# Unpacking w1 and w2 on three engines, ELU sums and every fourth gated product on ScalarE and GpSimd, and longer waits assumed in the scheduler's list

## The chip, the cores and the metric

The kernel is one program on 1 core of one Trainium2 chip. Its engines are called by the profile's names: PE is TensorE (matrix products), PEld its weight loads, DVE is VectorE, ACT is ScalarE, POOL is GpSimd, and SP issues the transfers. The metric is device time in microseconds (us); lower is better.

## What is computed

Top-k attention (32 largest of 576 scores a row) with 8 heads on 4 batches of 576 tokens, then an ELU layer, then a gated layer with two more products:

```python
def _attn_ref(q, k, v):                          # q, k, v: 4 x 8 x 576 x 64, float32
    scores = np.matmul(q, k.transpose(0, 1, 3, 2)) / np.sqrt(D)
    kth = np.partition(scores, -32, axis=-1)[..., -32:-31]
    scores = np.where(scores >= kth, scores, -1e9)
    attn = np.exp(scores - np.max(scores, axis=-1, keepdims=True))
    attn = attn / (np.sum(attn, axis=-1, keepdims=True) + 1e-09)
    return np.matmul(attn, v)

def _moe_ref(x, w_in, w_out):                    # x: 2304 x 512, d_ff 2048
    h = x @ w_in
    return np.where(h > 0, h, np.exp(np.minimum(h, 0)) - 1) @ w_out

def _moe2_ref(x, w1, w2, w3, w_out):             # 512 -> 1024, 1024 -> 1024, 1024 -> 512
    return (((x @ w1) * (x @ w2)) @ w3) @ w_out
```

The weights are float64 on the host and reach the kernel as pairs of 32-bit words.

## The kernel before, in words

**Tiles and chunks.** The 2304 tokens are 18 tiles of 128; `CHUNKS` makes 9 chunks of 2 tiles. Attention works on a tile and a pair of heads at a time, 72 such steps in all, called attention tiles below: 8 to a chunk. The layers behind attention (`mlp`) work on a chunk of 256 tokens.

**One attention tile.** PE computes the scores of one head into the single buffer `psS` (L376). ACT copies them to SBUF (L382). DVE finds the 32 largest by four MAX8 (L389) with three MATCH_REPLACE8 between them (L392), per head. ACT makes the masked exponentials (L409, L411) and their fp16 high half `pi` (L426), POOL the low half (L427), SP transposes them into `pt` (L429), PE multiplies with the values (L442, 28 matmuls, called AV below), DVE scales by the sum (L447), ACT and POOL split the result in halves (L449, L450), and SP transposes it into the chunk's input `x` (L451).

**One chunk of the layers.** Every product is made of three fp16 products (high by high, high by low, low by high). `unitA` (8 a chunk, L674 to L676) multiplies x with w_in and makes the ELU: Relu of the negated product, Exp (ACT, L686 and L687), a scale (POOL, L689), and the sum of both branches. For chunks 0 and 1 (`gm0`, `gm1` are 0) the sum is one DVE instruction (L691); for the others (`gm` is 1) ACT makes a Relu (L695) and POOL adds (L696). ACT and POOL split the result (L697, L698). `unitO` (8 a chunk, L711 to L713) multiplies with w_out into `psY`. `y_evac` copies the output of the ELU layer (ACT L723, DVE L724); the first copy of chunk 0 is called the first output copy below. `unitB` (8 a chunk, L753 to L755) multiplies with w1 and w2; the gated product is an ACT copy (L772) and a DVE product (L773), and ACT and POOL split it (L778, L779). `unitD` (2 a chunk, L788 to L790) multiplies with w34, the product of w3 and w_out made once at the start.

**Weights.** `load64` brings 128 x 512 pairs of words and turns them into float32. With `whole` it takes three DVE instructions (L474 to L476); otherwise ACT scales the low words (L478), DVE joins the two (L479), ACT takes the sign (L480) and POOL adds (L481). Before the change w1 and w2 (16 pieces, `w12`) go by the first way, all others (56 pieces) by the second. A norm over each weight sets its scale; `convert` then splits each piece into halves (ACT L503, and DVE L506 or PE L515 and L516 with ACT L518).

**What sets the order.** All work is first listed as operations with an engine, an assumed cost and a priority (`Program.op`). `emit` plays the list through: an engine that is free takes the operation with the lowest rank (priority less `cpw` times the length of the path behind it) of those whose inputs would be there by the assumed costs and by the waits in `LAT`, the time from one engine's end to another's start. The program is then written out in that order, and each engine runs its own instructions strictly in it. The numbers in `PAR` are the priorities: `a0`, `a1` shift the first attention chunks, `lag0`, `lag` the layers behind attention, `pi`, `po`, `p12`, `p34` the loads of the weights, `ci`, `co`, `c12`, `c34` their conversion.

## Time and profile before

| | before |
|---|---|
| time, median of 3 runs | 1086.86 us (1085.69 to 1093.07) |
| time of the profiled execution | 1089.24 us |
| its span, first to last instruction | 1087.5 us |
| mean granted TensorE clock | 0.968 of 2.4 GHz |
| PE busy | 984.1 us (90%), 9132 matmuls |
| DVE busy | 921.6 us (85%), 2002 instructions |
| ACT busy | 834.9 us (77%), 1729 instructions |
| POOL busy | 661.2 us (61%), 689 instructions |

A busy time is the time that an engine had an instruction in work, as a share of the span. Matmuls overlap, so their listed durations add up to more than their engine's busy time; so do those of DVE and ACT to a smaller part, since an instruction's listed time begins a little before the one ahead of it has ended. A wait is put down to the instruction that came last by the profile. PEclk is the granted clock of TensorE as a share of 2.4 GHz.

### The profile page before, as it was taken

Reading aid. Unit: us, or ns where it says so; the run is one execution under the profiler, and the core shown is the slowest. Engines: PE = TensorE matmul, PEld = TensorE weight load, DVE = VectorE, ACT = ScalarE, POOL = GpSimd, SP = SyncE. Lnnn points to the kernel's source line nnn. Section 1 sums busy time; section 2 is a strip of 40 time slices with the busy share of each in tenths; the row PEclk is TensorE's granted clock in tenths of the full one; section 3 lists DMA queues with packets and bytes.
Section 4 is the critical chain, followed back from the end, with each engine's and each line's share of the span. In section 5 each row is a group of like instructions: output and inputs, shape, how many; then the busy total and the mean of one; then the engine's idle time right before and its main releaser. Section 6 shows DMA issues by size and latency. Waiting matters only on the chain.

```text
span 1087.5 us, 24859 instructions
## 1 busy us (share of the span) xinstructions
PE 984.1 (90%) x9132; PEld 780.0 (72%) x9132; DVE 921.6 (85%) x2002; ACT 834.9 (77%) x1729; POOL 661.2 (61%) x689
## 2 busy tenths in 40 slices
PE   3489847889889999999999999999999999999998
PEld 2244524569678868877886887788879869878875
DVE  6999999899999999999996999998799999951011
ACT  6878797697878867897896798788878967953522
POOL 4898862256357735974794597458738845852711
PEclk9989968799899999999999999999999999999999
DMA  9999996554458895467859657665864563230000
GB/s 363 296 316 316 303 275 169 159 130 112 120 144 163 191 231 149 101 166 198 187 134 237 168 116 144 174 183 124 207 160 113 133 159 81 68 84 11 2 20 20
DMA packets 262298, 174.65 MB, mean 161 GB/s; under 512 B 197408, under 2 KB 224032, under 8 KB 262176
## 3 DMA queue, kind: packets, MB, share of 16 engines
q1 hardware_dynamic: 262176, 173.07, 60.3%
q8 instruction: 71, 1.16, 0.5%
q14 instruction: 51, 0.42, 0.1%
HBM read 104.33 MB, written 21.50 MB: 116 GB/s over the span
## 4 chain that ended last, share of the span: by engine, by line
DVE 22%; PE 14%; ACT 10%; POOL 8%; issue 5%; DMA 5%; SPq 1%; POOLq 0%; ACTq 0%; DVEq 0%
DVE m L389 10%; DVE wk L392 9%; DMA pt<-pi 3%; POOL pi L427 2%; PE psR L753 2%; PE psR L755 2%; PE psR L754 2%; ACT pi L426 2%; POOL g L698 1%; POOL t L696 1%; ACT y L411 1%; ACT s L382 1%; PE psR L788 1%; DMA qr<-qd 1%; PE psR L790 1%
## 5 line engine op out<-in xcount | busy, mean ns | idle before, releaser
L389 DVE MAX8 m<-wk 128x8 f32<-128x576 f32 x432 | 312.5, 747 | 1.3
L427 POOL TENSOR_TENSOR pi<-y,pi 128x576 f16<-128x576 f32 x144 | 188.0, 1314 | 126.6 <-ACT pi L426 96.8
L392 DVE MATCH_REPLACE8 wk<-m,wk 128x576 f32<-128x576 f32 x288 | 212.4, 741 | 0.0
L712 PE MATMUL psY<-g,wout 128*128 128x256 f16 x576 | 157.5, 273 | 1.9 <-POOL g L698 1.9
L753 PE MATMUL psR<-x,w 128*128 128x256 f16 x576 | 158.5, 275 | 0.8 <-DVE t L773 0.8
L754 PE MATMUL psR<-x,w 128*128 128x256 f16 x576 | 158.2, 275 | 1.1 <-DVE x L724 1.1
L674 PE MATMUL psR<-x,win 128*128 128x256 f16 x576 | 158.6, 275 | 0.1
L755 PE MATMUL psR<-x,w 128*128 128x256 f16 x576 | 158.3, 275 | 0.0
L711 PE MATMUL psY<-g,wout 128*128 128x256 f16 x576 | 157.7, 274 | 0.4 <-ACT g L697 0.4
L676 PE MATMUL psR<-x,win 128*128 128x256 f16 x576 | 158.0, 274 | 0.0
L675 PE MATMUL psR<-x,win 128*128 128x256 f16 x576 | 158.0, 274 | 0.0
L713 PE MATMUL psY<-g,wout 128*128 128x256 f16 x576 | 157.6, 274 | 0.0
L376 PE MATMUL psS<-kt,qh 128*128 128x288 f32 x320 | 110.2, 359 | 38.6 <-ACT s L382 19.1
L411 ACT ACTIVATE y<-y,ty 128x576 f32<-128x576 f32 x144 | 110.7, 771 | 3.3 <-POOL ty L401 3.3
L382 ACT ACTIVATE s<-psS 128x576 f32<-128x576 f32 (+1 forms) x160 | 102.3, 640 | 12.3 <-PE psS L376 11.4
L409 ACT ACTIVATE y<-s,ty 128x576 f32<-128x576 f32 x144 | 107.1, 769 | 5.4 <-POOL pi L427 2.1
L389 DVE MAX8 m<-s 128x8 f32<-128x576 f32 x144 | 105.1, 746 | 6.4 <-ACT s L382 6.0
L392 DVE MATCH_REPLACE8 wk<-m,s 128x576 f32<-128x576 f32 x144 | 106.3, 741 | 0.0
L376 PEld LDWEIGHTS psS<-kt,qh 128*128 128x128 f32 x320 | 63.4, 198 | 54.5 <-ACT s L382 24.7
L442 PE MATMUL psA<-vv,pt 128*128 128x64 f16 (+1 forms) x2240 | 84.1, 196 | 17.2 <-DMA pt<-pi 17.1
L442 PEld LDWEIGHTS <-pt 128*128 128x128 f16 (+1 forms) x2240 | 77.6, 103 | 29.8 <-DMA pt<-pi 20.4
L426 ACT ACTIVATE pi<-y 128x576 f16<-128x576 f32 x144 | 95.2, 677 | 3.8 <-DMA pt<-pi 3.4
(167 smaller groups left out, 2426.8 us busy)
## 6 DMA issues: line engine op xcount, KB each, us to landing
kt<-kd SPq DMA_DIRECT2D x64, 288.0 KB, 3.3
vv<-vd SPq DMA_DIRECT2D x32, 448.0 KB, 4.6
qr<-qd SPq DMA_DIRECT2D x72, 128.0 KB, 3.0
raw<-kd SPq DMA_DIRECT2D x32, 288.0 KB, 4.2
kd<-kt SPq DMA_DIRECT2D x32, 288.0 KB, 3.9
wout<-w_in SPq DMA_DIRECT2D x16, 512.0 KB, 8.3
w<-w3t SPq DMA_DIRECT2D x16, 512.0 KB, 7.0
w<-w_out SPq DMA_DIRECT2D x16, 512.0 KB, 6.2
```

The lines of the kernel that those rows point to most:

```text
L376: T.matmul(psS[:, half, 0:288], lhsT=L[qs][:, hh], rhs=KT[kk][:, half * 288:half * 288 + 288], start=li == 0, stop=li == 1)
L389: op("DVE", 685, lambda r=r, src=src, m8=m8, hh=hh: V.max(m8[:, hh, 8 * r:8 * r + 8], src), [skey], [mk], p1 + PAR["ot"] * STEP)
L392: op("DVE", 677, lambda r=r, nsrc=nsrc, w=w, m8=m8, hh=hh: V.match_replace(w, m8[:, hh, 8 * r:8 * r + 8], nsrc, -3.0e38), [skey, mk], [k], ...
L427: op("POOL", 1234, lambda Y=Y, PIs=PIs: G.tensor_tensor(PIs[:, S:2 * S], Y, PIs[:, 0:S], op=OP.subtract), [yk], [("pi", ps)], p4 + .034 * ...
L442: T.matmul(psA[c0:c1, hs], lhsT=PT[pts[hh]][:, j, c0:c1], rhs=W[vs][:, j, hs], start=i == 0, stop=i == 13)
L674: T.matmul(o, lhsT=hi(W)[:, cs], rhs=X[:, 0, kd_, 0:N], start=kd_ == 0, stop=False)
L675: T.matmul(o, lhsT=hi(W)[:, cs], rhs=X[:, 1, kd_, 0:N], start=False, stop=False)
L676: T.matmul(o, lhsT=lo(W)[:, cs], rhs=X[:, 0, kd_, 0:N], start=False, stop=kd_ == 3)
L711: T.matmul(o, lhsT=hi(W)[:, cs], rhs=rh, start=ft == 0 and m % 2 == 0, stop=False, skip_group_check=True)
L753: T.matmul(o, lhsT=hi(W)[:, cs], rhs=X[:, 0, kd_, 0:N], start=kd_ == 0, stop=False)
L754: T.matmul(o, lhsT=hi(W)[:, cs], rhs=X[:, 1, kd_, 0:N], start=False, stop=False)
L755: T.matmul(o, lhsT=lo(W)[:, cs], rhs=X[:, 0, kd_, 0:N], start=False, stop=kd_ == 3)
```

## The change

- `whole` no longer holds `w12`: the 16 pieces of w1 and w2 are unpacked by ACT, DVE, ACT and POOL (L478 to L481), and `WORD` halves their scale.
- `gm0` and `gm1` go from 0 to 1: the ELU sums of chunks 0 and 1 (16 units) go by L695 and L696.
- `bm` goes from 0 to 4: in units B 0 and 4 of each chunk (18 in all) ACT copies both products in one instruction (L766) and POOL multiplies them (L770).
- The waits in `LAT` between different engines are about 1.8 times as long, the assumed rate of a transfer falls from 360 to 325 bytes a ns, a few assumed costs change, and nearly all priorities have other values.

The core of the diff (the assumed costs of QK, AV, MAX8, MATCH_REPLACE8, the weight product, the conversion, the transposes, the norm's products and a matmul are left out; the norm's rises by 27%, each other changes by 16% or less):

```diff
-LAT = {("ACT", "PE"): 285.0, ("POOL", "PE"): 210.0, ("DVE", "PE"): 200.0, ("PE", "ACT"): 197.0, ("PE", "DVE"): 197.0, ("ACT", "ACT"): 153.0,
+LAT = {("ACT", "PE"): 513.0, ("POOL", "PE"): 378.0, ("DVE", "PE"): 360.0, ("PE", "ACT"): 355.0, ("PE", "DVE"): 355.0, ("ACT", "ACT"): 153.0,
...
-PAR = dict(whole=('w12',), cd={'wi': [0, 0], 'wo': [0, 0], 'w34': [8, 0], 'w12': [16, 0]}, pv=116.655, pi=265.308, p34=113.061, po=180.969, p12=190.557, pis=199.858,
+PAR = dict(whole=(), cd={'wi': [0, 0], 'wo': [0, 0], 'w34': [8, 0], 'w12': [16, 0]}, pv=230.352, pi=214.696, p34=-22.369, po=324.064, p12=151.752, pis=458.007,
...
-           nr34=2, gm0=0, gm1=0, gm=1, bm=0, cpw=13.0, step=6600.0, pvb=-52.296)
+           nr34=2, gm0=1, gm1=1, gm=1, bm=4, cpw=15.929, step=6600.0, pvb=-214.285)
...
-        op("SP", nbytes / 360.0, lambda: Q.dma_start(dst, src), r, w, pr, lat=475.0)
+        op("SP", nbytes / 325.0, lambda: Q.dma_start(dst, src), r, w, pr, lat=475.0)
```

How the order moves, at three places. First DVE, where pieces of w1 and w2 are unpacked, at the 9th attention tile before and the 10th now; `w` is the weight buffer, `pp` the buffer in which raw words and later the gated products stand, `m`, `wk` and `s` belong to attention. Before:

```order
L479 SCALAR_TENSOR_TENSOR w_115<-w_115 128x512
L474 TENSOR_SCALAR w_115<-w_115 128x512 x2
L475 SCALAR_TENSOR_TENSOR w_115<-w_115 128x512 x2
L476 SCALAR_TENSOR_TENSOR w_115<-w_115 128x512 x2
L474 TENSOR_SCALAR w_115<-pp 128x512
L447 TENSOR_TENSOR xf_156<-psA,ty_166 128x128
L475 SCALAR_TENSOR_TENSOR w_115<-pp,w_115 128x512
L474 TENSOR_SCALAR w_115<-pp 128x512
L476 SCALAR_TENSOR_TENSOR w_115<-pp,w_115 128x512
```

After:

```order
L389 MAX m_161<-s_134 128x8
L389 MAX m_160<-wk_137 128x8
L479 SCALAR_TENSOR_TENSOR pp<-pp 128x512
L392 MATCH_REPLACE wk_137<-m_160,wk_137 128x576
L288 TENSOR_REDUCE sc<-psY_170 128x1
L389 MAX m_160<-wk_137 128x8
L479 SCALAR_TENSOR_TENSOR pp<-pp 128x512
L447 TENSOR_TENSOR xf_156<-psA,ty_166 128x128
```

Three DVE instructions a piece have become one, with attention's instructions between one piece and the next.

Second ACT, at the 9th attention tile, where w_out is converted (`wout`, from the result `psY` of PE). Before:

```order
L400 ACTIVATE ty_164<-m_160 128x2
L409 ACTIVATE y_138<-s_132,ty_164 128x576
L409 ACTIVATE y_139<-s_133,ty_164 128x576
L503 ACTIVATE wout<-wout,sc 128x512 x2
L518 ACTIVATE wout<-psY_171 128x512
L382 ACTIVATE s_132<-psS 128x576
L518 ACTIVATE wout<-psY_170 128x512
L411 ACTIVATE y_138,ty_164<-y_138,ty_164 128x576
```

After:

```order
L411 ACTIVATE y_139,ty_164<-y_139,ty_164 128x576
L449 ACTIVATE xt_155<-xf_156 128x128
L426 ACTIVATE pi_141<-y_139 128x576
L478 ACTIVATE pp<-pp 128x512
L480 ACTIVATE w_115<-pp 128x512
L503 ACTIVATE wout<-wout,sc 128x512
L413 ACTIVATE ty_164<-ty_164 128x2
L503 ACTIVATE wout<-wout,sc 128x512 x2
L478 ACTIVATE pp<-pp 128x512
L480 ACTIVATE w_115<-pp 128x512
```

The unpacking of w1 and w2 (L478, L480) now stands on ACT between attention's copies and the conversion of w_out. Of ACT's instructions, 418 stood ahead of the first output copy (L723) before, and 477 stand there now: 32 of the 59 more are L478 and L480, 8 are L695, and 19 are others, since attention is one tile to two further at that place.

Third PE, right behind the last AV. Before:

```order
L442 LDWEIGHTS pt_143
L442 MATMUL psA<-vv_131,pt_143 128x64
L788 LDWEIGHTS pp
L788 MATMUL psR_174<-w_116,pp 128x512
L789 LDWEIGHTS pp
```

After:

```order
L442 LDWEIGHTS pt_143
L442 MATMUL psA<-vv_131,pt_143 128x64
L753 LDWEIGHTS w_115
L753 MATMUL psR_173<-x_145,w_115 128x256
L754 LDWEIGHTS w_115
L754 MATMUL psR_173<-x_145,w_115 128x256
```

Before, 18 matmuls of unit D and all 192 of chunk 7's units B followed the last AV; now 48 of these B matmuls do, and the other 144 and the 18 stand ahead of it. Up to the 56th attention tile the PE work ahead of each AV is almost what it was.

## Rows read from the trace of the kernel before

**Rows 1.** Busy time by stretch: stretch, its length, each engine's busy time (instructions), PEclk, DMA share, GB/s.
```profile
0.00:163.20 163.20, 107.61 (x529) 59.49 (x529) 146.23 (x265) 133.10 (x255) 125.17 (x104) 0.91 0.98 312
163.20:284.40 121.20, 104.25 (x881) 75.76 (x882) 115.61 (x272) 95.04 (x194) 53.79 (x57) 0.91 0.55 140
284.40:973.90 689.50, 662.42 (x6821) 557.28 (x6821) 647.11 (x1435) 569.85 (x1217) 447.82 (x496) 0.99 0.62 152
973.90:1087.50 113.60, 109.83 (x904) 87.45 (x900) 12.68 (x33) 36.91 (x65) 34.41 (x33) 1.00 0.04 16
```
**Rows 2.** ACT in order of time around the first output copy: start, duration, instruction.
```profile
282.93 0.67 ACT L723 ACTIVATE x<-psY,sc 128x512 f16<-128x512 f32 x1
283.50 1.46 ACT L503 ACTIVATE w<-w,sc 128x512 f16<-128x512 f32 x2
```
**Rows 3.** PE in order of time: the first unit B, and the end of the last AV.
```profile
287.21 0.27 PE L753 MATMUL psR<-x,w 128*128 128x256 f16 x1
...
973.36 0.58 PE L442 MATMUL psA<-vv,pt 128*128 128x64 f16 x14 [0.16 <-DMA pt<-pi]
```
**Rows 4.** ACT's waits up to 284.4 us: in total, times, longest.
```profile
ACT qh L356 <- DMA qr<-qd: 8.6, 2, 5.5
ACT ty L400 <- DVE m L389: 7.2, 5, 2.9
ACT w L618 <- PE psY L614: 5.9, 3, 2.9
ACT wout L503 <- DVE sc L263: 5.8, 1, 5.8
```
**Rows 5.** DVE groups by line: count, busy us, mean ns of one, idle before them.
```profile
L479 DVE SCALAR_TENSOR_TENSOR w<-w 128x512 int32<-128x512 int32 x40 | 37.3, 938 | 2.8 <-ACT w L478 2.6
L773 DVE SCALAR_TENSOR_TENSOR t<-psR,sc,t 128x256 f32<-128x256 f32 x72 | 34.0, 475 | 34.5 <-ACT t L772 34.3
L691 DVE SCALAR_TENSOR_TENSOR t<-psR,sc,t 128x512 f32<-128x512 f32 x16 | 11.7, 739 | 2.2 <-POOL t L689 2.2
L475 DVE SCALAR_TENSOR_TENSOR w<-pp,w 128x512 int32<-128x512 int32 x10 | 7.1, 707 | 0.0
L476 DVE SCALAR_TENSOR_TENSOR w<-pp,w 128x512 int32<-128x512 int32 x10 | 6.8, 682 | 0.0
L474 DVE TENSOR_SCALAR w<-pp 128x512 int32<-128x512 int32 x10 | 4.4, 441 | 4.3 <-DMA pp<-w 3.0 <-POOL g L481 1.2
```
**Rows 6.** Line L479 by itself: duration min/median/max in ns, first and last start.
```profile
L479 DVE SCALAR_TENSOR_TENSOR w<-w x40: 667/694/1792, 11.0 to 166.9; 128x512 int32<-128x512 int32 x40
L479 DVE SCALAR_TENSOR_TENSOR wout<-wout x16: 671/1101/1798, 13.2 to 122.2; 128x512 int32<-128x512 int32 x16
```
**Rows 7.** ACT groups by line.
```profile
L695 ACT ACTIVATE t<-psR,sc 128x512 f32<-128x512 f32 x56 | 38.2, 682 | 0.4 <-POOL g L698 0.4
L772 ACT ACTIVATE t<-psR,sc 128x256 f32<-128x256 f32 x72 | 33.6, 466 | 39.2 <-PE psR L755 35.0 <-DVE sc L263 4.0
L478 ACT ACTIVATE w<-w 128x512 int32<-128x512 uint32 x40 | 27.0, 674 | 5.1 <-DMA w<-w_out 2.9 <-POOL pi L427 1.3 <-DMA w<-w 0.7
```
**Rows 8.** POOL groups by line.
```profile
L696 POOL TENSOR_TENSOR t<-t,t 128x512 f32<-128x512 f32 x56 | 71.4, 1276 | 2.3
L357 POOL TENSOR_TENSOR ql<-qr,qh 128x256 fp32r<-128x256 f32 x72 | 53.9, 748 | 24.7 <-ACT qh L356 24.6
L481 POOL TENSOR_TENSOR pp<-pp,w 128x512 int32<-128x512 int32 x16 | 24.8, 1561 | 2.8 <-DVE w L479 2.7
```
**Rows 9.** PE's waits from 284.4 to 973.9 us.
```profile
PE psA L442 <- DMA pt<-pi: 10.9, 16, 2.1
PE psS L376 <- ACT s L382: 8.5, 10, 1.9
```
**Rows 10.** Pieces of the chain that ended last: start, length, what.
```profile
870.85 0.80 PE psS L376 x4
...
875.56 0.82 PE psA L442 x28
```

More of the change, by code (lines that the diff above doesn't have):

```diff
@@ L23 @@
 DM, DFF, DH = 512, 2048, 1024
-CHUNKS = [2]*9
-LAT = {("ACT", "PE"): 285.0, ("POOL", "PE"): 210.0, ("DVE", "PE"): 200.0, ("PE", "ACT"): 197.0, ("PE", "DVE"): 197.0, ("ACT", "ACT"): 153.0,
-       ("ACT", "DVE"): 147.0, ("ACT", "POOL"): 175.0, ("DVE", "ACT"): 128.0, ("DVE", "DVE"): 127.0, ("DVE", "POOL"): 203.0, ("POOL", "ACT"): 75.0,
-       ("POOL", "DVE"): 60.0, ("POOL", "POOL"): 88.0, ("PE", "PE"): 0.0, **{(e, "SP"): 67.0 for e in ("PE", "ACT", "DVE", "POOL")}}
+CHUNKS = [2] * 9
+LAT = {("ACT", "PE"): 513.0, ("POOL", "PE"): 378.0, ("DVE", "PE"): 360.0, ("PE", "ACT"): 355.0, ("PE", "DVE"): 355.0, ("ACT", "ACT"): 153.0,
+       ("ACT", "DVE"): 265.0, ("ACT", "POOL"): 315.0, ("DVE", "ACT"): 230.0, ("DVE", "DVE"): 127.0, ("DVE", "POOL"): 365.0, ("POOL", "ACT"): 135.0,
+       ("POOL", "DVE"): 108.0, ("POOL", "POOL"): 88.0, ("PE", "PE"): 0.0, **{(e, "SP"): 67.0 for e in ("PE", "ACT", "DVE", "POOL")}}
 NXS = 2
 STEEP = 2.0 ** 100
-PAR = dict(whole=('w12',), cd={'wi': [0, 0], 'wo': [0, 0], 'w34': [8, 0], 'w12': [16, 0]}, pv=116.655, pi=265.308, p34=113.061, po=180.969, p12=190.557, pis=199.858,
-           pos=-94.236, p12s=-194.985, p34s=16.277, ci=202.374, co=66.783, cos=-57.999, c12=275.249, m34=-471.595, c34=-63.018, m34s=28.657, h34=2, oq=53.713, os=7.994,
-           ok=113.472, ot=242.797, orr=151.048, opp=-250.875, oa=-82.219, ost=0.618, a0=125.007, a1=-15.227, lag0=114.106, lag=21.439, ho=2, h12=0, h12c=7,
-           nr34=2, gm0=0, gm1=0, gm=1, bm=0, cpw=13.0, step=6600.0, pvb=-52.296)
+PAR = dict(whole=(), cd={'wi': [0, 0], 'wo': [0, 0], 'w34': [8, 0], 'w12': [16, 0]}, pv=230.352, pi=214.696, p34=-22.369, po=324.064, p12=151.752, pis=458.007,
+           pos=-341.301, p12s=-225.683, p34s=41.293, ci=319.03, co=146.49, cos=-451.25, c12=177.354, m34=-791.931, c34=-287.596, m34s=53.079, h34=2, oq=63.603, os=43.99,
+           ok=226.416, ot=389.564, orr=844.424, opp=-269.728, oa=-91.857, ost=-258.2, a0=93.413, a1=30.072, lag0=93.126, lag=31.769, ho=2, h12=0, h12c=7,
+           nr34=2, gm0=1, gm1=1, gm=1, bm=4, cpw=15.929, step=6600.0, pvb=-214.285)
 def conv_modes(n, d, g):
@@ L286, in gram @@
                     T.matmul(ps[0:w, o:o + w], lhsT=c, rhs=c, start=pi == 0 and j == 0, stop=pi == len(pieces) - 1, skip_group_check=True)
-            op("PE", 55 * (n + 127) // 128, gram, keys, [pk], pr)
+            op("PE", 70 * (n + 127) // 128, gram, keys, [pk], pr)
         op("DVE", 600, lambda: V.tensor_reduce(m, ps, axis=AX.X, op=OP.max), [pk], ["nm0"], pr)
@@ L388, in attention @@
                         src, skey = (sS, ("s", ss)) if r == 0 else (w, k)
-                        op("DVE", 685, lambda r=r, src=src, m8=m8, hh=hh: V.max(m8[:, hh, 8 * r:8 * r + 8], src), [skey], [mk], p1 + PAR["ot"] * STEP)
+                        op("DVE", 665, lambda r=r, src=src, m8=m8, hh=hh: V.max(m8[:, hh, 8 * r:8 * r + 8], src), [skey], [mk], p1 + PAR["ot"] * STEP)
                         if r < 3:
                             nsrc = sS if r == 0 else w
-                            op("DVE", 677, lambda r=r, nsrc=nsrc, w=w, m8=m8, hh=hh: V.match_replace(w, m8[:, hh, 8 * r:8 * r + 8], nsrc, -3.0e38),
+                            op("DVE", 727, lambda r=r, nsrc=nsrc, w=w, m8=m8, hh=hh: V.match_replace(w, m8[:, hh, 8 * r:8 * r + 8], nsrc, -3.0e38),
                                [skey, mk], [k], p1 + PAR["ot"] * STEP)
@@ L428, in attention @@
                        [yk], [("pi", ps)], p4 + .034 * STEP)
-                    op("SP", 1008, lambda PIs=PIs, pt=pt: Q.dma_start_transpose(out=PT[pt], in_=PIs), [("pi", ps)], [("pt", pt)], p4 - 1e6, lat=1406.0)
+                    op("SP", 1050, lambda PIs=PIs, pt=pt: Q.dma_start_transpose(out=PT[pt], in_=PIs), [("pi", ps)], [("pt", pt)], p4 - 1e6, lat=1406.0)
                 if t == 0:
@@ L516, in rest @@
             T.matmul(ps, lhsT=nident, rhs=hi(W[i]), start=False, stop=True)
-        op("PE", 1080, rest, [*skeys, (nm, i), ("si", sid), "ident"], [pk], pr)
+        op("PE", 1250, rest, [*skeys, (nm, i), ("si", sid), "ident"], [pk], pr)
         op("ACT", 480, lambda: A.activation(lo(W[i]), ps, AF.Copy), [pk], [(nm, i, "l")], pr)
@@ L613, in part @@
                     k = a * 4 + kk
-                    op("PE", 860, lambda w=w3[a][0], kk=kk, k=k: T.matmul(acc, lhsT=w[:, kk * 128:kk * 128 + 128], rhs=W4[k][0], start=k == 0, stop=k == 7),
+                    op("PE", 930, lambda w=w3[a][0], kk=kk, k=k: T.matmul(acc, lhsT=w[:, kk * 128:kk * 128 + 128], rhs=W4[k][0], start=k == 0, stop=k == 7),
                        w3[a][1] + W4[k][1], [ak], p1)
@@ L659, in mlp @@
         N = n * 128
-        nm = N / 2.4 + 3.0
+        nm = N / 2.4 + 3.2
         pr_of = lambda u: pr0 + u * span / 28.0
@@ L791, in unitD @@
                 ks = [("pp", 2 * q), ("pp", 2 * q + 1), ("w34", 2 * q), ("w34", 2 * q + 1)]
-                op("PE", 1305, mm, ks + [k + ("l",) for k in ks], [("rot", rs)], pr)
+                op("PE", 1325, mm, ks + [k + ("l",) for k in ks], [("rot", rs)], pr)
             ts = nxt("t2", NT2)
```

4 lines of the change are left out of this document (2 added, 2 removed).

## The prediction

> **What bounds the kernel now.** I read the busy times by stretch first, then what each engine waited for, then the prices of the instructions that the change adds and removes.
>
> DVE sets the pace until attention is over. Up to 284.4 us it is busy 146.23 and 115.61 us, all but 22.6, and from there to the last AV 647.11 of 689.50, or 94% [rows 1]. PE is nearly as full in that second part: 662.42 of 689.50, 27.1 idle, at a granted share of 0.99 [rows 1]. What is left after the last AV at 974 is PE alone, 109.83 us busy of 113.60 [rows 1, 3]. So the span is made of two things: the time at which PE gets its first work behind the ELU layer (the first output copy at 282.9, the first unit B at 287.2 [rows 2, 3]), and from then on PE's own work plus the little that it loses. DVE's load matters only through those losses.
>
> ACT has room at the start: 133.10 and 95.04 us busy up to 284.4, so 56.3 idle. In the middle it is at 569.85 of 689.50, 83%. POOL has 105.4 us idle up to 284.4 [rows 1].
>
> **What each edit costs, engine by engine.**
>
> *DVE.* A piece of w1 or w2 took 441 + 707 + 682 ns by L474 to L476, 1.83 us; 16 pieces are 29.3 us that go. Each now takes one L479, at 938 ns on the mean: 15.0 come [rows 5]. The 16 ELU sums of 739 ns (11.8) and 18 gated products of 475 (8.6) go [rows 5]. Net: 34.7 us less. Of this little shows ahead of the first output copy, since by the order attention is further along there: -29.3 + 15.0 - 5.9 (8 ELU sums), but 11 MAX8, 6 MATCH_REPLACE8 and 3 conversions more, which at 0.74 to 0.8 us each (the 740 ns of the instructions of that size [rows 5]) are about 15. That is -5. The other 30 us leave the time between the first output copy and the end (1 of them after the last AV).
>
> The price of L479 is uncertain, because it swings: 667 ns at the least, 1792 at the most, and a median of 694 on one buffer, 1101 on another [rows 6]. By the median of 694 the 16 cost 11.1 us, by that of 1101 17.6. I keep 15.0; both ends move DVE's sum by 4 us at most.
> The Trainium skill (SBUF — State Buffer, Who interferes with whom) gives a reason: a VectorE instruction with two SBUF inputs and a GpSimd one that reads SBUF exclude each other, so that the later waits out the earlier. The spread of 667 to 1792 ns agrees; by this rule the new ones, beside a fuller GpSimd, would lie at 1101, and the net saving would be 32 us instead of 34.7.
>
> *ACT.* 16 pieces at two passes of 674 ns (L480 has the same shape) are 21.6 us, 16 Relus of 682 are 10.9, and 18 double copies at 682 instead of 466 are 3.9 [rows 7]. Listed durations overlap: the output copy of 0.67 us is followed after 0.57 [rows 2], so 0.10 goes from each of 48 new instructions. Sum: 36.4 - 4.8 = 32 us more.
> Ahead of the first output copy stand 59 more instructions: 32 unpacking passes at 0.57 (18.4), 8 Relus at 0.58 (4.7), and 19 of attention and conversion at the mean of all of ACT, 834.9 us over 1729 (9.2). That is 32 us, against 56.3 idle.
>
> *POOL.* 16 adds of 1561 ns (25.0), 16 ELU adds of 1276 (20.4), and 18 products of 128 x 256 at the 748 ns of the subtraction of that size (13.5) [rows 8]. That is 59 us more, 35 of it ahead of the first output copy, beside 105.4 idle [rows 1]. I cost it at nothing there; if the cover fails, rival 3 has the price.
>
> *SP and DMA.* The bytes are the same. The raw buffers of w1 and w2 are freed by POOL instead of DVE and the last loads stand later in the order; the early stretch moves 312 GB/s at a busy share of 0.98, and only the next, at 0.55 [rows 1], takes these loads. No term.
>
> *The list.* Longer assumed waits put dependent instructions further apart. That cannot shorten an instruction; it can only take idle time from engines whose queue heads wait. Nothing else hides in it.
>
> **The sum.** First, the first output copy. Its place on ACT needs ACT's work ahead of it, 227 us (133.10 + 95.04 less the 1.5 behind its start [rows 1, 2]), plus 32, plus the idle time that remains. Of the 56.3 us, waits for the loads of q (8.6), for the weight product (5.9) and for a scale (5.8) stay [rows 4]: 20 us as the lower bound. The upper bound is all 56. Waits for MAX8 (7.2 [rows 4]) and much of the small rest fall away, since ACT is now the later one there; I take 33, nearer the lower end. 227 + 32 + 33 = 292, **9 us later** (bounds -4 and +32).
>
> Second, 16 score matmuls and two AV groups more stand ahead of the first unit B. They cost 4 x 0.80 + 2 x 0.82 [rows 10], **4.8 us** that do not come later.
>
> Third, PE's losses from there to the last AV: 27.1 idle, and 0.01 of 689.5 at the lower clock, 6.9: 34 us [rows 1]. DVE, which drops from 647 to about 618 of 689.5 (90%), no longer paces PE in most places. But 10.9 of the idle time waits for the transposes of `pt` and 8.5 for ACT's score copies [rows 9], and those are not DVE's work. Bounds: 0 and 34 back; I take about half, **18**.
>
> 1087.5 + 9 - 4.8 - 18 = 1073.7 us of span. The profiled execution took 1.7 us more than its span and lies 2.4 above the median of the runs: **1073 us**, 1.3% faster. Note what this says of attention's end: behind the last AV stand 162 matmuls fewer (144 of B, 18 of D), which at 109.83 us for 904 [rows 1] is 19.7 us. So the last AV would end at about 981 instead of 974, although the whole is shorter.
>
> **Rivals.**
>
> 1. *ACT takes DVE's place.* ACT gets its 32 us exactly where the layers of chunk 0 hang on it (conversions of w_out, of w1 and w2, the ELU), and its queue is in order: idle time is not filled if the head waits. For it: ACT's order now has the unpacking between attention and conversion, and ACT is ahead of DVE only by that idle time. Against: of the 56.3 us only 20 are waits that I can name as fixed, and 83% later leaves room. Price: 42 us stay idle, so the copy is 18 later, DVE waits for score copies in the following ten tiles, and PE gets 11 back: 1087.5 + 18 - 4.8 - 11, **1089 us**, no change.
> 2. *DVE's relief goes through whole.* The copy comes 4 us earlier, where DVE's order lets it, and PE gets all 27.1 of idle time back, at the same clock: 1087.5 - 4 - 4.8 - 27.1, **1051 us**. For it: DVE at 94%. Against: the waits for `pt` [rows 9].
> 3. *GpSimd gets in the way, and the kernel is slower.* The 35 us put on POOL ahead of the first output copy stand in front of attention's low halves (L427), for which the transposes and so AV wait. For it: POOL was at 125.17 of 163.20 at the start [rows 1]. Against: only 53.79 of the next 121.20. If none of it is hidden: 1087.5 + 35 - 4.8 - 11, **1106 us**. It decides from a copy 27 us later, at 310: then the kernel is over 1% slower with 11 back. The Trainium skill (GPSIMD Engine Reference, Engine selection) sends elementwise additions and products to VectorE, since GpSimd takes about twice as long with two inputs. The trace agrees in the price: 682 + 1276 ns in place of 739 [rows 5, 7, 8]; whether it counts hangs on which engine is late.
>
> **How the numbers follow.** My sum 0.45, rival 1 0.30, rival 2 0.12, rival 3 0.13. The sum's own range is 1060 to 1084 (copy 4 earlier to 20 later, PE 10 to 27 back, not all at once). The range of 1053 to 1101 leaves out about half of rival 2 and most of rival 3. A measurement of this kernel can tell about 1% from no change, so 1076 and 1098 are the limits: faster 0.47 (three quarters of the sum, rival 2), same 0.34 (the rest of the sum, most of rival 1), slower 0.19 (rival 3, the far end of rival 1).
>
> **What would show it.** Right: DVE about 887 us busy, ACT 867, POOL 720; the first output copy between 285 and 301; PE's idle time from there to the last AV near 15 instead of 27; the last AV near 981 with about 94 us behind it. DVE's waits for the score copies (L382) may rise to 20 us in all. Wrong in the first step if the copy is later than 305 or earlier than 280; wrong in the third if PE's losses stay at 34, which with the copy 9 us later gives no change. A DVE sum above 900 would mean that L479 pays for GpSimd's load.

## The result, and the profile after

The changed kernel takes 1072.6 us in the median of 4 runs (1069.03 to 1074.64), the kernel before 1087.01 beside it. The ratio is 0.9837, with a 95% interval of 0.9808 to 0.9866. The profiled execution has a span of 1072.9 us instead of 1087.5, and a mean granted clock of 0.978 instead of 0.968.

Busy times of the changed kernel, from the page:

```profile
PE 974.6 (91%) x9132; PEld 776.8 (72%) x9132; DVE 907.8 (85%) x1936; ACT 863.4 (80%) x1777; POOL 714.9 (67%) x739
```

Busy times by stretch, cut at the first output copy and at the last AV as [rows 1] is, in the same columns:

```profile
0.00:163.20 163.20, 105.84 (x528) 59.22 (x529) 147.82 (x254) 133.51 (x253) 127.77 (x100) 0.94 0.94 300
163.20:296.00 132.80, 109.50 (x913) 77.89 (x912) 121.85 (x271) 125.27 (x256) 87.93 (x90) 0.91 0.60 161
296.00:979.60 683.60, 669.74 (x6971) 568.83 (x6968) 630.79 (x1395) 572.28 (x1216) 465.62 (x517) 1.00 0.63 151
979.60:1072.90 93.30, 89.52 (x731) 70.89 (x728) 7.30 (x19) 32.34 (x55) 33.54 (x33) 1.00 0.04 13
```

The first output copy on ACT, which answers to [rows 2]:

```profile
295.99 0.69 ACT L723 ACTIVATE x<-psY,sc 128x512 f16<-128x512 f32 x1
```

PE in order of time: the first unit B and the last AV, as in [rows 3]:

```profile
298.27 0.27 PE L753 MATMUL psR<-x,w 128*128 128x256 f16 x1
...
978.62 0.98 PE L442 MATMUL psA<-vv,pt 128*128 128x64 f16 x28
```

For the account, the kernel before has to be cut at its own copy, 1.5 us earlier than in [rows 1]:

```profile
0.00:282.90 282.90, 211.27 (x1396) 134.68 (x1396) 260.34 (x531) 226.67 (x445) 178.96 (x160) 0.91 0.80 239
282.90:973.90 691.00, 663.00 (x6835) 557.84 (x6836) 648.61 (x1439) 571.32 (x1220) 447.82 (x496) 0.99 0.62 152
```

From these rows the 14.6 us of span come out whole. The copy is 13.1 later (296.0 against 282.9). PE has 4.1 more of its work behind it by then (215.34 against 211.27). From the copy to the last AV it stands idle 683.60 - 669.74 = 13.9 us instead of 691.00 - 663.00 = 28.0, so 14.1 come back. Behind the copy PE's busy time falls from 663.00 + 109.83 to 669.74 + 89.52, by 13.6; 4.1 of that is the work done earlier, and 9.5 is the same 9132 matmuls taking less time over the whole span. The mean granted clock, which rose, would give just that (984.1 x 0.968 / 0.978 = 974.0, and 974.6 was measured), but the same sum fails for a kernel in the same order: for unpack_held below it gives 974.6 x 0.978 / 0.973 = 979.6, and 973.3 was measured. So how much of the 9.5 is the clock is not shown; the last section has a reason why that mean is not to be leaned on. Sum: 13.1 - 4.1 - 14.1 - 9.5 = -14.6. The 20 us by which the stretch behind the last AV is shorter are not a gain by themselves: those matmuls now stand ahead of it.

What PE waits for between the copy and the last AV (in total, times, longest), against [rows 9]:

```profile
PE psA L442 <- DMA pt<-pi: 8.4, 13, 2.0
PE psS L376 <- DMA kt<-kd: 3.9, 2, 2.8
```

The waits for the score copies, 8.5 us before, are gone, and those for `pt` fell from 10.9 to 8.4.

### The profile page after: what moved, and what is told of

Its sections match the earlier page's. It is cut to its first block, busy times and chain, and to the rows that moved or that the text cites. A ratio compares the mean times of both kernels' runs of the same rounds, so it can differ in the third digit from the quotient of the medians.

```text
span 1072.9 us, 24950 instructions
## 1 busy us (share of the span) xinstructions
PE 974.6 (91%) x9132; PEld 776.8 (72%) x9132; DVE 907.8 (85%) x1936; ACT 863.4 (80%) x1777; POOL 714.9 (67%) x739
## 4 chain that ended last, share of the span: by engine, by line
PE 45%; ACT 16%; DVE 14%; DMA 10%; issue 9%; POOL 6%; SPq 1%; POOLq 0%; ACTq 0%; DVEq 0%
DMA pt<-pi 5%; DVE m L389 4%; PE psS L376 4%; DVE wk L392 4%; PE psR L753 4%; PE psR L754 4%; PE psR L755 4%; PE psR L674 4%; PE psR L676 4%; PE psR L675 4%; PE psA L442 3%; PE psY L711 3%; PE psY L712 3%; PE psY L713 3%; DVE w L479 2%
## 5 line engine op out<-in xcount | busy, mean ns | idle before, releaser
L389 DVE MAX8 m<-wk 128x8 f32<-128x576 f32 x432 | 314.1, 748 | 2.4
L376 PE MATMUL psS<-kt,qh 128*128 128x288 f32 x320 | 109.8, 358 | 37.0 <-POOL kt L308 25.1
L389 DVE MAX8 m<-s 128x8 f32<-128x576 f32 x144 | 105.9, 747 | 23.4 <-ACT s L382 22.8
L382 ACT ACTIVATE s<-psS 128x576 f32<-128x576 f32 (+1 forms) x160 | 102.7, 642 | 19.3 <-PE psS L376 18.1
L376 PEld LDWEIGHTS psS<-kt,qh 128*128 128x128 f32 x320 | 63.3, 198 | 49.6 <-POOL kt L308 27.6
```

What stands on the lines that cost most here:

```text
L376: T.matmul(psS[:, half, 0:288], lhsT=L[qs][:, hh], rhs=KT[kk][:, half * 288:half * 288 + 288], start=li == 0, stop=li == 1)
L389: op("DVE", 665, lambda r=r, src=src, m8=m8, hh=hh: V.max(m8[:, hh, 8 * r:8 * r + 8], src), [skey], [mk], p1 + PAR["ot"] * STEP)
```

## The experiments

All numbers of a profile are from one execution each; the ratios are from repeated runs beside the kernel before. "Copy" is the start of the first output copy, "idle" PE's idle time from there to the last AV, "DVE" its busy time in the same stretch with its share.

| kernel | ratio to before, 95% | span | copy | last AV | idle | DVE |
|---|---|---|---|---|---|---|
| before | 1 | 1087.5 | 282.9 | 973.9 | 28.0 | 648.6 (94%) |
| after | 0.9837 (0.9808 to 0.9866) | 1072.9 | 296.0 | 979.6 | 13.9 | 630.8 (92%) |
| work_only | 1.1048 (1.1 to 1.1095) | 1198.3 | 420.1 | 1086.1 | 26.7 | 560.4 (84%) |
| list_only | 1.0628 (1.0587 to 1.0669) | 1150.7 | 395.6 | 1058.5 | 7.7 | 588.4 (89%) |
| waits_only | 1.0192 (1.0122 to 1.0261) | 1105.7 | 302.1 | 994.8 | 28.8 | 641.3 (93%) |
| short_waits | 1.0782 (1.0718 to 1.0847) | 1168.6 | 407.0 | 1075.2 | 12.1 | 587.1 (88%) |
| nudge | 1.0056 (1.0033 to 1.0079) | 1092.1 | 305.8 | 998.8 | 19.0 | 643.2 (93%) |
| dve_less | 0.9972 (0.994 to 1.0004) | 1083.3 | 284.8 | 969.8 | 26.1 | 628.9 (92%) |
| dve_less_after | 0.9826 (0.9772 to 0.988) | 1065.5 | 297.2 | 972.3 | 7.0 | 609.7 (90%) |
| early_less | 0.9951 (0.9923 to 0.9978) | 1079.8 | 279.3 | 966.2 | 25.8 | 648.0 (94%) |
| unpack_held | 0.9999 (0.9975 to 1.0024) | 1085.9 | 312.3 | 992.7 | 11.9 | 632.5 (93%) |
| no_add | 0.9844 (0.9801 to 0.9888) | 1065.9 | 292.0 | 972.6 | 11.7 | 630.9 (93%) |
| no_add_scale | 0.981 (0.9765 to 0.9856) | 1064.0 | 290.7 | 970.7 | 11.2 | 631.8 (93%) |
| elu_less | 0.9825 (0.9785 to 0.9864) | 1064.3 | 294.1 | 971.1 | 9.2 | 631.0 (93%) |

In the first four runs, work_only to short_waits, the scheduler plays out a new order. In nudge it does too, from a number changed by half a per cent. In the last seven the order of either kernel is held, instruction by instruction, and some are left out or replaced.

How far two executions differ by themselves can be read from the same runs. The spans of the kernel before go from 1078.1 to 1090.8 in 19 executions, those of the changed kernel from 1067.2 to 1072.9 in four. In dve_less nothing ahead of the copy differs from the kernel before, yet the copy is 1.9 us later and DVE 4.0 us longer busy by then. Differences of that size between two profiles show nothing.

### Work alone, list alone

The kernel before with the changed work and its own numbers (work_only):

```diff
-PAR = dict(whole=('w12',), cd={'wi': [0, 0], 'wo': [0, 0], 'w34': [8, 0], 'w12': [16, 0]}, pv=116.655, pi=265.308, p34=113.061, po=180.969, p12=190.557, pis=199.858,
+PAR = dict(whole=(), cd={'wi': [0, 0], 'wo': [0, 0], 'w34': [8, 0], 'w12': [16, 0]}, pv=116.655, pi=265.308, p34=113.061, po=180.969, p12=190.557, pis=199.858,
...
-           nr34=2, gm0=0, gm1=0, gm=1, bm=0, cpw=13.0, step=6600.0, pvb=-52.296)
+           nr34=2, gm0=1, gm1=1, gm=1, bm=4, cpw=13.0, step=6600.0, pvb=-52.296)
```

> The three moves of work alone: w1 and w2 unpacked on three engines, ELU sums of chunks 0 and 1 and every fourth gated product on ScalarE and GpSimd, with all waits, costs and priorities of before. My theory is that the time comes from VectorE's relief behind the first output copy, less what ScalarE loses ahead of it. Then this alone gives most of the gain: 1074 to 1080 us, with PE idle for less than 20 us from the first output copy to the last AV (27.1 before), and that copy 8 to 20 us later than 282.9. The rival is that the new list of waits and priorities makes the gain, and that the moved work only costs: then 1087 to 1095 us and PE's idle time there stays at 25 us or more.

The changed kernel's numbers with the work of before (list_only) is the same edit to the changed kernel in the other direction: `whole=('w12',)`, `gm0=0`, `gm1=0`, `bm=0`.

> The other half: all waits, costs and priorities of after, and the work where it was before (w1 and w2 unpacked by VectorE in three instructions, ELU sums of chunks 0 and 1 and all gated products on VectorE). My theory: VectorE is as full as before, so PE loses 25 us or more behind the first output copy, and the time is 1081 to 1090 us. The rival that the list makes the gain: 1068 to 1076 us. If both halves give half each, the time is near 1080 us in both runs.

Measured: 10.5% and 6.3% slower, both far above every range that was expected. Each half by itself loses over 60 us, although together they gain 14. Both lose it ahead of the first output copy, which comes at 420.1 and 395.6. Line L389 ahead of the copy, in the kernel before, in work_only and in list_only (min/median/max in ns, first and last start; six such instructions make an attention tile):

```profile
L389 DVE MAX8 m<-wk x88: 730/746/761, 18.4 to 280.1; 128x8 f32<-128x576 f32 x88
```

```profile
L389 DVE MAX8 m<-wk x140: 732/747/764, 18.4 to 415.5; 128x8 f32<-128x576 f32 x140
```

```profile
L389 DVE MAX8 m<-wk x123: 734/746/762, 17.2 to 372.3; 128x8 f32<-128x576 f32 x123
```

Before, 14.7 attention tiles are through DVE at that point; in the half-changed kernels it is 23.3 and 20.5, so the chunk-0 layers have slipped behind six to nine more attention tiles, where a chunk has eight. No instruction has become dearer (746, 747 and 746 ns): the list plays the same kind of work in another order. In the middle the two part. Busy times from the copy to the last AV, work_only and then list_only:

```profile
420.10:1086.10 666.00, 639.32 (x6503) 538.82 (x6504) 560.39 (x1220) 514.30 (x1084) 428.08 (x474) 0.99 0.54 131
```

```profile
395.60:1058.50 662.90, 655.18 (x6718) 555.47 (x6717) 588.40 (x1307) 525.46 (x1121) 420.70 (x466) 1.00 0.57 139
```

With the lighter DVE (84%) and the list of before PE idles 26.7 us, about as much as before. With the heavier one (89%) and the new list it idles 7.7. That speaks against DVE's load as the cause of the 14 us, and for the list.

### Which part of the list

The longer waits alone, in the kernel before (waits_only), the six lines of `LAT` taken over; the first:

```diff
-LAT = {("ACT", "PE"): 285.0, ("POOL", "PE"): 210.0, ("DVE", "PE"): 200.0, ("PE", "ACT"): 197.0, ("PE", "DVE"): 197.0, ("ACT", "ACT"): 153.0,
+LAT = {("ACT", "PE"): 513.0, ("POOL", "PE"): 378.0, ("DVE", "PE"): 360.0, ("PE", "ACT"): 355.0, ("PE", "DVE"): 355.0, ("ACT", "ACT"): 153.0,
...
```

> The kernel before with the longer waits between engines alone (about 1.8 times), all else as before. If the longer waits keep queue heads from waiting, PE's waits for the transposes (10.9 us) and for score copies (8.5 us) behind the first output copy fall, and the time is 1075 to 1083 us. My theory says that waits of 0.1 to 0.2 us more in the list do not decide there, since VectorE is full: 1083 to 1095 us.

The changed kernel with the shorter waits of before (short_waits) is the same edit backwards.

> The kernel after with the shorter waits between engines of before in the list, all else as after. PE's waits for score copies behind the first output copy were 8.5 us before and none after. If the longer waits are what keeps PE from waiting there, they come back here (over 5 us) and PE's idle time from the copy to the last AV is 22 us or more; if the priorities do, it stays under 16 us. The whole time can be anything from 1070 to 1120 us, as waits_only (1107) shows, since the first output copy moves with any change of the list.

Measured: 1.9% and 7.8% slower, both above the ranges that were expected. What PE waits for from the copy to the last AV, waits_only and then short_waits:

```profile
PE psA L442 <- DMA pt<-pi: 15.4, 19, 2.5
PE psS L376 <- ACT s L382: 7.8, 12, 2.3
```

```profile
PE psA L442 <- DMA pt<-pi: 6.1, 13, 1.3
PE psS L376 <- DMA kt<-kd: 2.1, 1, 2.1
...
PE psS L376 <- ACT s L382: 1.0, 3, 0.4
```

The longer waits do not take the idle time away (28.8 us of it, with 7.8 for score copies), and with the shorter ones and the new priorities it stays away (12.1, with 1.0). So it is the rest of the list, the priorities together with the assumed costs and the transfer rate, that keeps PE fed in the middle; it is called "the priorities" below. With the shorter waits the time is lost at the start: the copy at 407.0.

How firm that is, one more order tells: the changed kernel with `cpw` half a per cent higher (nudge).

```diff
-           nr34=2, gm0=1, gm1=1, gm=1, bm=4, cpw=15.929, step=6600.0, pvb=-214.285)
+           nr34=2, gm0=1, gm1=1, gm=1, bm=4, cpw=16.0, step=6600.0, pvb=-214.285)
```

> The kernel after with one number of the list changed by half a per cent (the weight of the path behind an operation, 15.929 to 16.0), so that no work and no cost moves, only the order. If the list's numbers are fitted closely, as work_only and list_only suggest, the first output copy moves by 5 us or more to either side and the time leaves 1073 by more than 8 us; if the order is sound in itself, the time stays within 5 us.

```profile
0.00:305.80 305.80, 222.45 (x1425) 138.43 (x1426) 266.31 (x516) 257.79 (x504) 211.19 (x190) 0.91 0.75 228
305.80:998.80 693.00, 673.99 (x6981) 571.28 (x6981) 643.17 (x1403) 576.11 (x1219) 465.83 (x517) 0.99 0.63 150
```

These are nudge's busy times up to the copy and from there to the last AV. The same instructions take 19 us more of span: the copy is 9.8 later, though DVE, ACT and POOL each had slightly less busy time ahead of it than in the changed kernel, and PE idles 5.1 more. The whole gain of the change is smaller than what a re-ordering that nobody would notice in the diff gives away. The middle keeps part of the advantage (19.0 idle against 28.0); so "the priorities" means this order, not a rule that any list near it would follow.

### Less of DVE behind the copy

In the order of before, the third MATCH_REPLACE8 of the second head is left out in five tiles of eight from chunk 2 on, 35 instructions (dve_less):

```diff
-                            op("DVE", 677, lambda r=r, nsrc=nsrc, w=w, m8=m8, hh=hh: V.match_replace(w, m8[:, hh, 8 * r:8 * r + 8], nsrc, -3.0e38),
+                            op("DVE", 677, (lambda: None) if r == 2 and hh == 1 and c >= 2 and (t * 4 + pair) % 3 else lambda r=r, nsrc=nsrc, w=w, m8=m8, hh=hh: V.match_replace(w, m8[:, hh, 8 * r:8 * r + 8], nsrc, -3.0e38),
```

> The kernel before in its very order, with 35 MATCH_REPLACE8 of chunks 2 to 8 left out (the third one of the second head, in five of eight attention tiles): about 26 us less for VectorE, all of it behind the first output copy, and nothing else changed (the values found after it differ a little). My theory is that VectorE paces PE there at 94 per cent busy: PE's idle time from the first output copy to the last AV falls from 27.1 to 10 to 18 us and the kernel ends 8 to 18 us earlier, 1069 to 1079 us. If VectorE does not pace PE (transposes, score copies and PE's own work do), the time stays within 3 us of before.

The same edit in the changed kernel's order (dve_less_after):

> The kernel after in its very order, with the 35 MATCH_REPLACE8 of dve_less left out (26 us less for VectorE behind the first output copy). If PE's own work bounds that part, as dve_less says for before, the time is 1069 to 1073 us; if VectorE, which now waits longer for score copies, paces it, 1055 to 1064 us.

From the copy to the last AV, dve_less and then dve_less_after:

```profile
284.80:969.80 685.00, 658.92 (x6835) 556.38 (x6836) 628.87 (x1369) 571.22 (x1220) 447.58 (x496) 0.99 0.63 154
```

```profile
297.20:972.30 675.10, 668.12 (x6986) 568.20 (x6984) 609.74 (x1326) 572.72 (x1216) 464.59 (x517) 1.00 0.63 153
```

In the order of before DVE is 19.7 us lighter, even a little more than the change made it there (17.8), and PE's idle time goes from 28.0 to 26.1. DVE then waits for PE instead. Its waits for the AV in the same stretch (12.5 us in the kernel before):

```profile
DVE xf L447 <- PE psA L442: 19.7, 14, 3.4
```

In the new order 21.0 us less give 6.9 of idle time back by the profile; the ratios (0.9826 against 0.9837) do not tell the two kernels apart. DVE's relief behind the copy is thus worth between nothing and about 7 us per 20, and in the old order PE got 2 of the 14 by it, which is no more than two executions can differ; by the ratio, dve_less took between nothing and 6.5 us off the time.

### What sets the first output copy

In the changed kernel's order w1 and w2 are unpacked by DVE again, in three instructions at the place where GpSimd's add stood (unpack_held); L478, L479 and L480 are left out for these pieces, and `WORD` gives them the scale of before:

```diff
-        op("POOL", 1255, lambda: G.tensor_tensor(d, d, low, op=OP.add), rk + wk, key, pr)
+        op("POOL", 1255, (lambda: (V.tensor_scalar(d, high, 3, 0x3FFFFFFF, op0=OP.logical_shift_left, op1=OP.bitwise_and), V.scalar_tensor_tensor(d, high, -0x40000000, d, op0=OP.bitwise_and, op1=OP.bitwise_or), V.scalar_tensor_tensor(d, low, 29, d, op0=OP.logical_shift_right, op1=OP.bitwise_or))) if nm == "w12" else lambda: G.tensor_tensor(d, d, low, op=OP.add), rk + wk, key, pr)
```

> The kernel after in its very order on PE and SP, with w1 and w2 unpacked by VectorE again: the four instructions on ScalarE, VectorE, ScalarE and GpSimd are left out and the three VectorE instructions of before stand where GpSimd's add stood. VectorE gets 16 x (1.83 - 1.05), about 13 us, ScalarE loses 18 and GpSimd 25, all ahead of the first output copy. If VectorE sets the time of that copy (my first theory), the copy comes 5 to 13 us later than 296 and the end with it: 1078 to 1086 us. If ScalarE sets it, the copy comes 5 to 15 us earlier: 1058 to 1068 us. If the fit of the order alone matters and the engines of this work do not, the time stays within 4 us of 1073.

```profile
0.00:312.30 312.30, 215.31 (x1452) 138.77 (x1453) 289.80 (x555) 242.29 (x475) 195.38 (x174) 0.91 0.75 224
312.30:992.70 680.40, 668.47 (x6954) 566.75 (x6953) 632.52 (x1396) 571.70 (x1216) 465.93 (x517) 1.00 0.62 152
```

Up to the copy DVE has 20.1 us more, ACT 16.5 less and POOL 20.3 less, and the copy comes 16.3 later. So with this load DVE sets it. Three instructions in a row make ACT wait; its longest wait up to the copy, 5.5 us in all in the changed kernel and 7.2 in [rows 4], is here:

```profile
ACT ty L400 <- DVE m L389: 26.4, 8, 13.2
```

Behind the copy nothing changes (11.9 idle), and the end is 13.0 later: 0.9999 of the time before. Putting the unpacking back, in an order that was planned without it there, costs the whole gain; an order fitted to it was not tried. The Trainium skill (GPSIMD Engine Reference, Engine selection) would have had the elementwise work on VectorE; the run that puts it there is 1.6% slower than the one that spreads it, since VectorE then becomes the later engine ahead of the copy.

That DVE sets the copy in the changed kernel too does not follow: the run adds to DVE, and none takes work from it ahead of the copy in this order. The changed kernel's own waits up to the copy, ACT's and then DVE's, speak for no single engine:

```profile
ACT ty L400 <- DVE m L389: 5.5, 5, 3.3
ACT kt L307 <- DMA raw<-kd: 5.1, 1, 5.1
ACT pp L478 <- DMA pp<-w: 4.1, 4, 1.9
```

```profile
DVE m L389 <- ACT s L382: 8.0, 7, 2.7
...
DVE ty L414 <- ACT ty L413: 3.4, 4, 1.8
```

In all ACT waits there 10.1 us for DVE and 17.3 for loads, DVE 14.4 for ACT. The chain of work, followed back from the first output copy to 100 us by the profile's rule, says the same: 69 us of ACT, 45 of DVE, 24 of PE and 24 of transfers in the changed kernel, but 97 of DVE and 16 of ACT before, and 128 of DVE and 41 of ACT in unpack_held.

Two runs take the price of the spreading away from the other engines, in the same order. First GpSimd's 16 adds alone (no_add):

```diff
-        op("POOL", 1255, lambda: G.tensor_tensor(d, d, low, op=OP.add), rk + wk, key, pr)
+        op("POOL", 1255, (lambda: None) if nm == "w12" else lambda: G.tensor_tensor(d, d, low, op=OP.add), rk + wk, key, pr)
```

> The kernel after in its very order, with GpSimd's 16 adds of w1 and w2 left out (25 us; these weights are then only their signs). If GpSimd is in the way ahead of the first output copy (rival 3), the copy comes 5 us or more earlier than 296 and the end with it, 1068 us or less; if GpSimd's idle time covers them, the time stays within 3 us of 1073. VectorE's join (L479) of these pieces no longer runs beside these adds: if its length of 1.05 us on the mean comes from GpSimd's adds, the pieces in pp and w fall to about 0.7 us.

```diff
-        op("ACT", 565, lambda: A.activation(low, low.bitcast(U32), AF.Copy, scale=2.0 ** -29 * (1 - 2.0 ** -9), bias=7.5 * 2.0 ** -9 - 0.5), rk, wk, pr)
+        op("ACT", 565, (lambda: None) if nm == "w12" else lambda: A.activation(low, low.bitcast(U32), AF.Copy, scale=2.0 ** -29 * (1 - 2.0 ** -9), bias=7.5 * 2.0 ** -9 - 0.5), rk, wk, pr)
```

> As no_add, and ScalarE's 16 scaling passes of the low words (L478) are left out too: 9 us less for ScalarE ahead of the first output copy, in the same order. If ScalarE's load sets the time of that copy, it comes 5 to 9 us earlier than in no_add and the end follows by as much: 1063 to 1068 us. If the copy waits for other things (loads, weight product, norms), the time is that of no_add within 3 us.

Up to the copy, no_add and then no_add_scale:

```profile
0.00:292.00 292.00, 216.58 (x1452) 138.38 (x1453) 265.98 (x523) 258.33 (x507) 195.89 (x174) 0.92 0.78 240
```

```profile
0.00:290.70 290.70, 215.21 (x1452) 138.16 (x1453) 265.04 (x523) 249.69 (x491) 197.10 (x174) 0.92 0.79 241
```

(no_add_scale leaves out ACT's 16 scalings, L478, as well.) 19.8 us less on POOL bring the copy 4.0 forward, and a further 8.6 less on ACT bring 1.3. ACT is covered there almost entirely, POOL to about four fifths; the 1.3 is within what two executions differ by. The spans are 7.0 and 8.9 shorter than the changed kernel's; the ratios, 0.9844 and 0.981, do not tell these kernels from the changed one.

The ELU sums of chunks 0 and 1, with L695 and L696 of these chunks left out (elu_less):

```diff
-                op("POOL", 150 + f2 * 2.1, lambda: G.tensor_tensor(t, t, t2a, op=OP.add), [t2k], [tk], pr)
+                op("POOL", 150 + f2 * 2.1, (lambda: None) if c < 2 else lambda: G.tensor_tensor(t, t, t2a, op=OP.add), [t2k], [tk], pr)
```

> The kernel after in its very order, with the ELU sums of chunks 0 and 1 left out (16 Relus of ScalarE, 11 us, and 16 adds of GpSimd, 20 us; these two chunks then lack the positive branch). Half of it stands ahead of the first output copy. If this work costs time there, the copy comes 3 to 5 us earlier and the end 3 to 8 us: 1065 to 1070 us; if it is covered, within 3 us of 1073.

The copy is 1.9 earlier and PE idles 4.7 less; the ratio is again within the interval of the changed kernel's. That is an upper bound: by the spans, the two instructions that took the place of one DVE instruction cost 8.6 us at most.

Last, the same question in the order of before: two of the three DVE instructions that unpack a piece of w1 or w2 are left out, 32 in all (early_less). The second of the two lines, the other is edited alike:

```diff
-            op("DVE", 602, lambda: V.scalar_tensor_tensor(d, low, 29, d, op0=OP.logical_shift_right, op1=OP.bitwise_or), rk, key, pr, lk=True)
+            op("DVE", 602, (lambda: None) if nm == "w12" else lambda: V.scalar_tensor_tensor(d, low, 29, d, op0=OP.logical_shift_right, op1=OP.bitwise_or), rk, key, pr, lk=True)
```

> The kernel before in its very order, with the second and third unpacking instruction (L475, L476) of the 16 pieces of w1 and w2 left out (these weights then have the exponent's lower part alone): 23 us less for VectorE, all ahead of the first output copy, nothing else changed. It is the counterpart of dve_less, where 26 us less behind that copy gave 4 us. If VectorE's load ahead of the copy is what the kernel pays, the copy comes 12 to 20 us earlier than 282.9 and the end 10 to 20 us: 1067 to 1077 us. If ScalarE or the loads take over at once, the gain is under 6 us.

Busy times up to the copy, and two of the waits between 160 us and the copy:

```profile
0.00:279.30 279.30, 212.16 (x1396) 135.10 (x1396) 242.29 (x499) 227.13 (x446) 175.10 (x160) 0.90 0.79 242
```

```profile
DVE w L474 <- DMA pp<-w: 9.0, 4, 6.3
...
ACT win L518 <- PE psY L516: 6.7, 6, 3.6
```

DVE has 18.1 us less ahead of the copy, and the copy is 3.6 earlier. DVE now waits for the loads of w1 and w2, 9.0 us where it was 3.0 [rows 5], and ACT for PE (6.7 us, 4.8 before). In the order of before DVE had others close behind it. This run and unpack_held are not mirror images: one takes work from DVE in the old order, the other adds to it in the new. What less of DVE ahead of the copy would bring in the new order was not tried.

## Why the prediction was right, and where it was not

**The time.** 1073 was forecast and 1072.6 measured. The picture of two parts held: when PE gets its first work behind the ELU layer, and what PE loses from there on. That the number came within 1 us is luck in part: the first two terms came out 4.8 us worse than forecast, the third 5.6 better.

**DVE's cost.** The sum was 34.7 us less; the listed durations fell by 26.3 (1038.2 to 1011.9 over all of DVE's groups) and the busy time by 13.8, to 907.8 instead of 887. Of the 20.9 us that are missing, 12.5 are overlap, to which the prediction gave no price on DVE although it took it off ACT's sum, 5.0 are the price of L479, and the other 3.4 are spread over small groups. The groups of L479 in the changed kernel, which answer to [rows 5], and the line by itself, which answers to [rows 6]:

```profile
L479 DVE SCALAR_TENSOR_TENSOR w<-w 128x512 int32<-128x512 int32 x44 | 45.3, 1034 | 0.4 <-ACT w L478 0.4
...
L479 DVE SCALAR_TENSOR_TENSOR wout<-wout 128x512 int32<-128x512 int32 x16 | 18.2, 1175 | 0.0
...
L479 DVE SCALAR_TENSOR_TENSOR pp<-pp 128x512 int32<-128x512 int32 x12 | 11.3, 941 | 1.8 <-ACT pp L478 1.7
```

```profile
L479 DVE SCALAR_TENSOR_TENSOR w<-w x44: 666/955/1808, 13.5 to 177.7; 128x512 int32<-128x512 int32 x44
L479 DVE SCALAR_TENSOR_TENSOR wout<-wout x16: 669/1164/1899, 11.4 to 122.6; 128x512 int32<-128x512 int32 x16
L479 DVE SCALAR_TENSOR_TENSOR pp<-pp x12: 666/693/1653, 127.5 to 233.3; 128x512 int32<-128x512 int32 x12
```

Count times mean gives 75.6 us for the 72, against 55.6 for the 56 of before (40 of 938 and 16 of 1130 ns): 20.0 more, not 15.0. Shared among the 16 new ones that is 1.25 us each, above the upper bound of 1101 ns, but the 12 on `pp` took only 941: the 44 on `w`, of which 40 had been there, went from a median of 694 to 955. As for the overlap, instructions that stand back to back lose a little of their listed time, and that came to 104 us in all instead of 117. The sign set for L479, a DVE sum above 900, was thus met, but mostly for another reason. Ahead of the copy the forecast was -5, and DVE got 9.3 us more busy time (269.67 against 260.34). Attention stood as much further along as forecast (11 MAX8 and 6 MATCH_REPLACE8 more), so the 14 us are others: 5 of L479, and 3 of lost overlap, since the listed durations rose by 6.3; the rest was not split.

**The first output copy (term 1).** 9 us later was forecast, 13.1 came, well within the bounds. ACT's work ahead of the copy rose by 32 us, as forecast (226.67 to 258.79), and its idle time was 37 us, forecast at 33. But that idle time was made of other waits than the prediction named: of the 20 us that it held to be fixed 6.7 remained (3.1 for the load of q, 3.6 for the weight product), and 12.0 for other loads stood beside them (5.1 on `raw`, 4.1 on `pp`, 2.8 on `w`). The reason given, ACT as the later engine, is borne out by the chain (69 us of ACT, 45 of DVE) and by DVE's waits for ACT, but not by the price: 8.6 us less of ACT's work (no_add_scale against no_add) moved the copy by only 1.3, while 20 more on DVE with ACT relieved (unpack_held) moved it by 16.3. What sets the copy in the changed kernel stays open.

**The matmuls moved ahead (term 2).** 4.8 forecast, 4.1 measured.

**PE's losses (term 3).** 18 back was forecast, 23.6 came: 14.1 of idle time and 9.5 of busy time (little of the 9.5 can lie ahead of the copy: the weight product, L614, took 4.7 us less there, and the conversion's products, L515 and L516, took 4.4 more). Idle 13.9 against the forecast of about 15. The failed step is its reason, "DVE, which drops from 647 to about 618 of 689.5 (90%), no longer paces PE". DVE dropped only to 630.8 of 683.6, and dve_less shows that such a drop by itself gives 2 us back in the old order. The prediction said of the list that nothing else hides in it; in fact the new priorities are what removed PE's waits for score copies (8.5 to 0). Every order by the priorities of before idles 25.8 to 28.8 us there, with DVE between 84 and 94% busy; every order by the new ones idles 7.0 to 19.0, with DVE between 88 and 93%. So the number was about right by a wrong cause, and that is luck: taking idle time from heads of queues was named as the one thing that the list could do, and then given no price.

**The end.** The last AV was forecast at 981 with about 94 behind it (the prediction's own terms add up to 980); 979.6 and 93.3 were measured. ACT 863.4 against 867, POOL 714.9 against 720. Of the prices behind POOL's sum the ELU adds at 1286 ns and the products at 730 held, and on ACT 683 for a double copy, as [rows 7, 8] had them. The adds of the unpacking, costed at 1561, took about 1.3 us each (ten of them are the line on `w<-w,pp`), which is 4 of the 5 us that POOL is below the forecast:

```profile
L696 POOL TENSOR_TENSOR t<-t,t 128x512 f32<-128x512 f32 x72 | 92.5, 1286 | 4.2 <-DVE m L389 0.9 <-ACT t L695 0.8
...
L770 POOL TENSOR_TENSOR t<-t 128x256 f32<-128x256 f32 x18 | 13.1, 730 | 29.4 <-ACT t L763 29.3
L481 POOL TENSOR_TENSOR w<-w,pp 128x512 int32<-128x512 int32 x10 | 12.9, 1293 | 13.6 <-DVE sc L263 4.3 <-ACT qh L356 2.3 <-DVE sc L262 1.8
...
L763 ACT ACTIVATE t<-psR,sc 128x512 f32<-128x512 f32 x18 | 12.3, 683 | 13.4 <-DVE sc L263 8.6 <-PE psR L755 4.8
```

The double copy stands at L763 in the trace; the text on the change called it L766.

**The rivals.** *ACT takes DVE's place* had the right sign of its marker: DVE's waits for the score copies rose from 6.0 to 22.8 us over the span, 14.9 of them behind the copy:

```profile
DVE m L389 <- ACT s L382: 14.9, 12, 2.6
```

What they cost was not measured by itself; 21 us less of DVE there gave PE 6.9 back (dve_less_after). *DVE's relief goes through whole* fails with the copy, 13.1 us later and not 4 earlier, and with the 13.9 us that remain, 8.4 of them for `pt`. *GpSimd gets in the way*: 19.8 us less on it ahead of the copy are worth 4.0 there, so neither nothing, as costed, nor all.

**What stays open.** Which of the some thirty changed priorities and costs removes the score-copy waits was not separated. Nor was it tried whether a list fitted to the work of before could reach the middle of the changed kernel with a copy at 283, which would be faster than both; none of the runs that compute the whole beats the changed kernel.

## What to carry to other kernels

Where a planner sets the order, cost an edit with the order held and the new order by itself: here either half alone was 6 to 11% slower, and half a per cent on one weight of the planner cost more than the whole gain. Read such a kernel as the time of the first dependent work plus what the full engine loses after it, and ask for each loss which engine's queue head is waiting, since relieving the busiest engine returns little where the order makes it wait elsewhere. Adding work to an engine does not price taking it off: 20 us more on DVE made the first output copy 16 us later in one order, 18 us less made it 4 earlier in another, where others stood close behind.
